# Top-k attention and SwiGLU FFN: attention straight through for nine units, the first block by halves, rounding in two VectorE steps

## The chip, the core and the metric

The kernel runs on one core of one Trainium2 chip. Its engines are named as in the profile: PE (TensorE, with PEld for its weight loads), DVE (VectorE), ACT (ScalarE), POOL (GpSimd) and SP (SyncE, which issues all transfers here). The metric is the device time in microseconds (us); lower is better. The time before is the median of three runs. A profile is one further execution; its span runs from its first to its last instruction.

## What is computed

Attention in which each query keeps its 32 highest scores, over 8 batches, 8 heads, 576 positions and head size 64; then a SwiGLU FFN on the 4608 x 512 result.

```python
scores = scale * np.matmul(q, k.transpose(0, 1, 3, 2))
kth = np.partition(scores, -top_k, axis=-1)[..., -top_k:-top_k + 1]
scores = np.where(scores >= kth, scores, -1000000000.0)
scores = scores - np.max(scores, axis=-1, keepdims=True)
attn = np.exp(scores)
attn = attn / (np.sum(attn, axis=-1, keepdims=True) + 1e-09)
x = bridge(np.matmul(attn, v))          # (B,H,S,D) -> (B*S, H*D)
g = x @ w_gate
silu = g * (1.0 / (1.0 + np.exp(-g)))
out = (silu * (x @ w_val)) @ w_out      # 4608x512 @ 512x1536, then 1536x512
```

The three weight matrices arrive as 64-bit floats and are brought to float32 inside the kernel, by integer operations on their two halves.

## The kernel before

**Units.** The attention is cut into 160 units, in the order batch, query tile, pair of heads: 8 batches, five query tiles (four of 128 queries, one of 64), four head pairs. A unit of a full tile does two heads one after the other on 128 partitions; a unit of the last tile holds both heads on the partition halves and counts as one head.

**One iteration of the main loop** (L523) selects for unit n on DVE, and carries its neighbours through the later stages on the other engines:

- `select(n)` (L264): four rounds of `max` (L277, the 8 highest) with three `match_replace` between them (L281), then one tensor_scalar (L287) that writes a penalty to `e` for every score below the 32nd. These eight steps are called one by one, with other work issued between them.
- `penalize(n-1)` (L291): on POOL, `e` + scores (L299). `weigh(n-1)` (L302): the exponential with its sum on ACT (L308). `normalize(n-1)` (L314): an addition and a reciprocal on DVE (L318, L320), and two multiplications on ACT (L323), which are issued at the start of the next iteration.
- `scores(n+1)` (L226): matrix products, copied out of PSUM by ACT.
- `turn(n-2)` (L325): nine transposes of `e` on PE with three copies on ACT (L336). `values(n-3)` (L346): attention times V, copied by ACT into `xT` (L379).
- `fetch(n+2)` (L492): transposes K and Q of a new head pair, or loads the next ones.

So unit n is finished in iteration n+3.

**FFN.** A block is 256 columns (tokens) of `xT`; 18 blocks. `feed(kb)` (L404) does it in 36 pieces: 24 of four matmul instructions (L418; two pieces make one product of 256 rows of gate or value) and 12 of two (L452, the output). A float32 matmul instruction shows as two records in the trace. Behind each product stand ACT instructions (L436 to L438 for a gate, L443 for a value) and a multiplication on POOL (L439, L444); they are kept in the lists `on_act` and `on_pool` and issued by later calls. `pieces(n)` issues up to n pieces if `credit` allows: each iteration adds 4.6 (2.3 for a unit of the last tile), at most 8.0 are kept. A block is begun when all its columns are there: block 0 needs units 0 to 7, block 1 units 8 to 15. What is left after the last unit runs in `while piece()` (L571).

**Rounding the weights.** The weights come in 72 pieces of 128 x 256 (`weights`, L129). Each goes through `rounded` (L92) in stages, and `rounding(k)` makes k steps; step i issues the load of piece i, the ACT and POOL part of piece i-3, the first DVE part of piece i-4 with POOL's addition, and the last DVE part of piece i-5. A step has three DVE instructions (L114, L117, L124), two on POOL (L102, L121) and two on ACT (L107, L109). In the first ten iterations there are five steps an iteration, two of them side by side, then four. `need` makes steps at once when a product wants a piece that isn't ready.

**Loads.** Before the loop, K and Q of the first four head pairs (`load`, six transfers each) and V (`load_v`, four each) are queued on SP, with three weight loads among them.

**Order.** The last loop (L579) chains every instruction of PE, DVE, ACT and POOL to the one issued before it: each engine works in the order in which the program issues. So an instruction that waits holds everything behind it on its engine.

Of the kernel before, what the change touches and what calls it, by code (L numbers as in the profile page):

```python
# [15 lines left out]
P = 128  # L16
# [4 lines left out]
BLK = 256  # L21
WP = 256
HUGE = 122880.0
LEAST = 3.4332275390625e-05


@with_exitstack
def kernel(
# [63 lines left out]
    def rounded(src, dst):  # L92

        n = dst.shape[1]
        w = ffn.tile([P, n, 2], I32, tag="w", name="w", bufs=4)
        nc.sync.dma_start(w[:], src.bitcast(I32).rearrange("p (f t) -> p f t", t=2))
        yield
        low, high = w[:, :, 0], w[:, :, 1]


        hi = conv.tile([P, n], FP32, tag="hi", name="hi")
        nc.gpsimd.tensor_scalar(  # L102
            hi[:], high.bitcast(FP32), HUGE, -HUGE, ALU.min, ALU.max
        )

        ulps = conv.tile([P, n], I32, tag="ulps", name="ulps")
        nc.scalar.mul(ulps[:], low.bitcast(U32), 2.0**-29)  # L107
        size = conv.tile([P, n], FP32, tag="size", name="size")
        nc.scalar.activation(size[:], hi[:], AF.Abs)  # L109
        yield  # L110

        hi = hi[:].bitcast(I32)
        bits = conv.tile([P, n], I32, tag="bits", name="bits")
        nc.vector.tensor_scalar(  # L114
            bits[:], hi, 3, 0x3FFFFFFF, ALU.logical_shift_left, ALU.bitwise_and
        )
        nc.vector.scalar_tensor_tensor(  # L117
            out=bits[:], in0=hi, scalar=-0x40000000, in1=bits[:],
            op0=ALU.bitwise_and, op1=ALU.bitwise_or,
        )  # L120
        nc.gpsimd.tensor_tensor(bits[:], bits[:], ulps[:], ALU.add)  # L121
        yield

        nc.vector.scalar_tensor_tensor(  # L124
            out=dst, in0=size[:], scalar=LEAST, in1=bits[:].bitcast(FP32),
            op0=ALU.is_ge, op1=ALU.mult,
        )

    def weights():  # L129
# [134 lines left out]
    def select(n):  # L264

        nh = n_heads(units[n][1])
        sc = state[n]["sc"]
        m = small.tile([P, 2, TOP_K], FP32, tag="m", name="m")
        heads = [slice(t * S, (t + 1) * S) for t in range(nh)]
        rest = work.tile([P, 2 * S], FP32, tag="rest", name="rest", bufs=1)  # L270
        e = work.tile([P, 2 * S], FP32, tag="e", name="e", bufs=3)
        state[n] |= dict(m=m, e=e, heads=heads)
        cur = sc
        rounds = TOP_K // 8
        for r in range(rounds):
            for t, hs in enumerate(heads):
                nc.vector.max(m[:, t, 8 * r : 8 * r + 8], cur[:, hs])  # L277
# [126 lines left out]
    def feed(kb):  # L404

        x = xT.pop(kb)
        hs = []  # L410

        def product(w, s, then):
            ps = ps_f.tile([P, 2, BLK], FP32, tag="f", name="f")
            need(8 * s + (4 if w is wg else 8))
            for i in range(2):
                m = 2 * s + i
                for c in range(KC):
                    nc.tensor.matmul(  # L418
                        ps[:, i, :],
                        w[:, c, m * P : (m + 1) * P],  # L420
                        x[:, c, :],
                        start=(c == 0),
                        stop=(c == KC - 1),
                    )
                if i == 1:
                    on_act.append(lambda: then(ps))
                yield

        for s in range(MS):
            h = ffn.tile([P, 2, BLK], FP32, tag="h", name="h", bufs=MS + 1)  # L430
            hs.append(h)


            def gate(ps, h=h):
                half = ffn.tile([P, 2, BLK], FP32, tag="gv", name="half_g", bufs=3)
                nc.scalar.activation(h[:], ps[:], AF.Tanh, scale=0.5)  # L436
                nc.scalar.mul(half[:], ps[:], 0.5)
                nc.scalar.add(h[:], h[:], 1.0)  # L438
                on_pool.append(lambda: nc.gpsimd.tensor_mul(h[:], h[:], half[:]))  # L439

            def value(ps, h=h):
                val = ffn.tile([P, 2, BLK], FP32, tag="gv", name="val", bufs=3)
                nc.scalar.copy(val[:], ps[:])  # L443
                on_pool.append(lambda: nc.gpsimd.tensor_mul(h[:], h[:], val[:]))  # L444

            yield from product(wg, s, gate)
            yield from product(wv, s, value)
        for t in range(BLK // P):
            ps = ps_f.tile([P, DM], FP32, tag="f", name="o_ps")
            for m in range(MC):  # L450
                need(8 * MS + 2 * m + 2)
                nc.tensor.matmul(  # L452
                    ps[:],
                    hs[m // 2][:, m % 2, t * P : (t + 1) * P],
                    wo[:, m, :],
                    start=(m == 0),
                    stop=(m == MC - 1),
                )
                if m == MC - 1:

                    def finish(ps=ps, t=t):
                        o = ffn.tile([P, DM], FP32, tag="o", name="o")
                        nc.scalar.copy(o[:], ps[:])
                        store(o, kb * BLK + t * P)

                    on_act.append(finish)
                if m % 2 == 1:
                    yield

    NU = len(units)  # L470
    todo = list(range(NBLK))
# [2 lines left out]
    def piece():  # L474

        if len(on_act) > 1:
            flush(on_act)
        if len(on_pool) > 1:
            flush(on_pool)
        while True:  # L480
            if not current:
                if not todo or done.get(todo[0], 0) < NHP * BLK:
                    return False
                flush(on_act)
                flush(on_pool)
                current.append(feed(todo.pop(0)))
            if next(current[0], 0) == 0:
                current.pop()
                continue
            return True  # L490

    def fetch(n):  # L492

# [5 lines left out]
            load(i + NHP)  # L499

    def pieces(n):
        for _ in range(n):
            if credit[0] >= 1 and piece():
                credit[0] -= 1

    def run(steps):
        for _ in steps:
            pass

    load(0)  # L510
    rounding(3)
    load(1)
    for i in range(NHP):
        if i > 1:
            load(i)
        load_v(i)
    run(fetch(0))
    run(scores(0))
    run(fetch(1))
    credit = [0.0]  # L520
    no = iter(())
    over = {}
    for n in range(NU + 3):  # L523
        topk = select(n) if n < NU else no
        over[n - 1] = normalize(n - 1) if 0 <= n - 1 < NU else no
        nxt = scores(n + 1) if n + 1 < NU else no
        turned = turn(n - 2) if 0 <= n - 2 < NU else no
        ahead = fetch(n + 2) if n + 2 < NU else no
        if n < NU:
            credit[0] = min(credit[0] + (2.3 if units[n][1] == J else 4.6), 8.0)  # L530
        flush(on_act)
        if 0 <= n - 1 < NU:
            penalize(n - 1)
        run(over.pop(n - 2, no))
        flush(on_pool)
        if n >= 3:
            values(n - 3)
            b, qt, hp = units[n - 3]
            if qt == J and b + 1 < B:
                load_v((b + 1) * NHP + hp)  # L540
        next(nxt, None)
        next(topk, None)
        next(topk, None)
        rounding(1 + (n < 2 * NHP + 2))
        pieces(1)
        next(nxt, None)
        next(turned, None)
        flush(on_act)
        pieces(1)
        next(turned, None)  # L550
        flush(on_act)
        if 0 <= n - 1 < NU:
            weigh(n - 1)
        flush(on_pool)
        next(topk, None)
        next(topk, None)
        rounding(1)
        next(ahead, None)
        pieces(1)
        next(ahead, None)  # L560
        next(topk, None)
        rounding(1)
        next(over[n - 1], None)
        pieces(1)
        next(topk, None)
        rounding(1)
        next(over[n - 1], None)
        next(topk, None)
        next(topk, None)
        pieces(6)  # L570
    while piece():  # L571
# [49 lines left out]
```

## Time and profile before

| | us |
|---|---|
| median of 3 runs (lowest, highest) | 1972.86 (1972.39, 1973.78) |
| the profiled execution | 1975.04 |
| its span | 1973.2 |
| PE busy | 1779.5 |
| DVE busy | 1640.1 |
| ACT busy | 1156.0 |
| POOL busy | 773.0 |

A line of the timeline gives start, length, engine, source line, operation, names and shapes; in brackets the idle time of the engine before it and what ended that. A line of the table by stages gives the stretch, its length, each engine's busy time and number of instructions, the clock granted to PE (1.00 is full), and the share and rate of DMA. The page draws the span in 40 slices of 49.3 us, a digit being tenths:

```profile
PE   3444779989999999999999999989999999899899
DVE  5999687998889998989799898998898988889700
POOL 2555453424334434343434352434343434243412
PEclk6566789999999999999999999999999999999999
DMA  5222111100030002100030002000120002000000
```

### The profile page before, as it was taken

Reading aid. Unit: us, or ns where it says so; the run is one execution under the profiler, and the core shown is the slowest. Engines: PE = TensorE matmul, PEld = TensorE weight load, DVE = VectorE, ACT = ScalarE, POOL = GpSimd, SP = SyncE. Lnnn points to the kernel's source line nnn. Section 1 sums busy time; section 2 is a strip of 40 time slices with the busy share of each in tenths; the row PEclk is TensorE's granted clock in tenths of the full one; section 3 lists DMA queues with packets and bytes.
Section 4 is the critical chain, followed back from the end, with each engine's and each line's share of the span. In section 5 each row is a group of like instructions: output and inputs, shape, how many; then the busy total and the mean of one; then the engine's idle time right before and its main releaser. Section 6 shows DMA issues by size and latency. Waiting matters only on the chain.

```text
span 1973.2 us, 29487 instructions
## 1 busy us (share of the span) xinstructions
PE 1779.5 (90%) x10144; PEld 1297.7 (66%) x10144; DVE 1640.1 (83%) x3708; ACT 1156.0 (59%) x2821; POOL 773.0 (39%) x686
## 2 busy tenths in 40 slices
PE   3444779989999999999999999989999999899899
PEld 1223655847686867686768686858686867586666
DVE  5999687998889998989799898998898988889700
ACT  3555455656575656666667566656675656565512
POOL 2555453424334434343434352434343434243412
PEclk6566789999999999999999999999999999999999
DMA  5222111100030002100030002000120002000000
GB/s 153 84 80 75 43 50 43 44 12 1 9 79 11 1 12 57 30 1 11 4 78 7 12 2 68 18 11 1 33 54 11 1 14 50 11 1 11 1 11 11
DMA packets 111253, 59.58 MB, mean 30 GB/s; under 512 B 89088, under 2 KB 97280, under 8 KB 111104
## 3 DMA queue, kind: packets, MB, share of 16 engines
q1 hardware_dynamic: 111104, 57.70, 11.1%
q8 instruction: 80, 1.31, 0.3%
q14 instruction: 69, 0.57, 0.1%
HBM read 48.23 MB, written 9.44 MB: 29 GB/s over the span
## 4 chain that ended last, share of the span: by engine, by line
PE 78%; DVE 13%; issue 3%; ACT 3%; POOL 2%; SPq 1%; DMA 1%; POOLq 0%; ACTq 0%; DVEq 0%
PE f L418 37%; PE o_ps L452 18%; PE av L364 7%; PE etps L335 6%; PE s L256 6%; DVE m L277 5%; DVE rest L281 4%; PE s L242 2%; PE av L355 1%; PE kqps L211 1%; DVE bits L117 1%; DVE e L287 1%; DVE bits L114 1%; ACT e L308 1%; POOL bits L121 1%
## 5 line engine op out<-in xcount | busy, mean ns | idle before, releaser
L299 POOL TENSOR_TENSOR e<-e,sc 128x1152 f32<-128x1152 f32 (+1 forms) x160 | 383.0, 2394 | 731.3 <-DVE e L287 487.1
L277 DVE MAX8 m<-rest 128x8 f32<-128x576 f32 x864 | 613.7, 747 | 2.2
L418 PE MATMUL f<-xT,wg 128*128 128x256 f32 x1728 | 423.1, 391 | 16.7 <-ACT xT L379 16.7
L281 DVE MATCH_REPLACE8 rest<-m,rest 128x576 f32<-128x576 f32 x576 | 423.9, 743 | 0.0
L418 PE MATMUL f<-xT,wv 128*128 128x256 f32 x1728 | 409.3, 384 | 0.0
L452 PE MATMUL o_ps<-wo,h 128*128 128x512 f32 x864 | 400.1, 599 | 4.4 <-DVE wo L124 4.4
L418 PEld LDWEIGHTS f<-xT,wg 128*128 128x128 f32 x1728 | 323.4, 194 | 89.7 <-issue 27.8
L336 ACT COPY et<-etps 128x512 f32<-128x512 f32 (+1 forms) x448 | 195.1, 477 | 305.8 <-PE etps L335 305.2
L418 PEld LDWEIGHTS f<-xT,wv 128*128 128x128 f32 x1728 | 321.0, 193 | 48.3 <-issue 9.9
L335 PE MATMUL etps<-ident,e 128*128 128x128 f32 (+1 forms) x1312 | 207.4, 289 | 122.2 <-ACT sc L261 70.5
L335 PEld LDWEIGHTS etps<-ident,e 128*128 128x128 f32 (+1 forms) x1312 | 168.0, 148 | 202.8 <-issue 99.1
L323 ACT ACTIVATE e<-e,tot 128x576 f32<-128x576 f32 x288 | 209.5, 770 | 133.7 <-DVE tot L320 133.7
L452 PEld LDWEIGHTS o_ps<-wo,h 128*128 128x128 f32 x864 | 153.6, 190 | 163.6 <-issue 156.0
L439 POOL TENSOR_TENSOR h<-h,half_g 128x512 f32<-128x512 f32 x108 | 137.9, 1277 | 265.3 <-ACT h L438 258.8
L308 ACT ACTIVATE e<-e,bias 128x576 f32<-128x576 f32 x288 | 221.6, 776 | 4.1 <-POOL e L299 4.1
L277 DVE MAX8 m<-sc 128x8 f32<-128x576 f32 x288 | 205.1, 749 | 10.1 <-ACT sc L261 10.1
L281 DVE MATCH_REPLACE8 rest<-m,sc 128x576 f32<-128x576 f32 x288 | 212.0, 743 | 0.0
L256 PE MATMUL s<-kqT 64*128 64x288 f32 x1024 | 172.7, 459 | 11.4 <-ACT kqT L216 11.3
L364 PE MATMUL av<-et,v 128*64 128x128 f32 (+1 forms) x2560 | 178.5, 281 | 2.1 <-ACT et L336 1.0
L261 ACT COPY sc<-s 128x288 f32<-128x288 f32 x512 | 167.2, 416 | 12.8 <-PE s L256 12.3
L318 DVE TENSOR_SCALAR tot<-tot 128x2 f32<-128x2 f32 (+1 forms) x160 | 25.4, 159 | 168.0 <-ACT e L308 168.0
L444 POOL TENSOR_TENSOR h<-h,val 128x512 f32<-128x512 f32 x108 | 139.1, 1288 | 60.7 <-ACT val L443 60.3
(45 smaller groups left out, 1459.8 us busy)
## 6 DMA issues: line engine op xcount, KB each, us to landing
kq_in<-in_k_dram SPq DMA_DIRECT2D x64, 128.0 KB, 2.8
kq_in<-in_q_dram SPq DMA_DIRECT2D x64, 128.0 KB, 3.0
v<-in_v_dram SPq DMA_DIRECT2D x32, 256.0 KB, 3.0
w<-in_moe_w_gate_dram SPq DMA_DIRECT2D x24, 256.0 KB, 2.7
w<-in_moe_w_val_dram SPq DMA_DIRECT2D x24, 256.0 KB, 2.7
w<-in_moe_w_out_dram SPq DMA_DIRECT2D x24, 256.0 KB, 2.5
out_dram<-o SPq DMA_DIRECT2D x40, 128.0 KB, 2.4
out_dram<-o SPq DMA_DIRECT2D x16, 256.0 KB, 2.4
```

The source lines that it names most:

```text
L256: nc.tensor.matmul(ps[:, 0:half], slab[d, q0 : q0 + P], slab[d, k0 : k0 + half])
L261: nc.scalar.copy(sc[:, i * half : (i + 1) * half], ps[:, 0:half])
L277: nc.vector.max(m[:, t, 8 * r : 8 * r + 8], cur[:, hs])
L281: nc.vector.match_replace(rest[:, hs], m[:, t, 8 * r : 8 * r + 8], cur[:, hs], LOWEST)
L299: nc.gpsimd.tensor_tensor(e[:, every], e[:, every], sc[:, every], ALU.add)
L308: nc.scalar.activation(e[:, hs], e[:, hs], AF.Exp, bias=bias[:, t : t + 1], scale=scale, accum_out=tot[:, t : t + 1],)
L323: nc.scalar.mul(e[:, hs], e[:, hs], tot[:, t : t + 1])
L335: nc.tensor.transpose(ps[0:kl, c * P : (c + 1) * P], e[:, k0 : k0 + kl], ident[:])
L336: nc.scalar.copy(et[0:kl, c0 : c0 + cn, :], ps[0:kl, 0 : cn * P].rearrange("p (c j) -> p c j", c=cn),)
L364: nc.tensor.matmul(av[hh * R : (hh + 1) * R, 0:ql], v_last[:, hh, :] if c == J else vt[:, hh, c, :], moving, start=last and c == 0, stop=c ...
L418: nc.tensor.matmul(ps[:, i, :], w[:, c, m * P : (m + 1) * P], x[:, c, :], start=(c == 0), stop=(c == KC - 1),)
L452: nc.tensor.matmul(ps[:], hs[m // 2][:, m % 2, t * P : (t + 1) * P], wo[:, m, :], start=(m == 0), stop=(m == MC - 1),)
```

## The change

- **Rounding.** The clamp moves behind the absolute value: ACT takes the absolute value first (L101 of the new kernel), POOL clamps it between LEAST and HUGE (L103), DVE shifts and masks (L110), POOL adds (L114), and one DVE instruction (L117) puts sign and top bit back from the loaded data. DVE has two instructions a step instead of three. LEAST is 2^-15 now. A loaded piece is held until its last step, and its ring has six buffers instead of four.
- **Steps.** In the first nine iterations (`head`) there are five calls of `rounding` instead of four, the new one between the first `max` and the first `match_replace`; each makes two steps in iterations 0 to 4, one after that. Four steps are made before the loop instead of three.
- **Straight through.** In the first nine iterations, unit n-1 is normalized, turned, multiplied with V and finished at the end of iteration n. Units from 8 on go the old way.
- **First block by halves.** Block 0 begins when units 0 to 3 are done, with its first 128 columns: 24 pieces of half width, then the same for the other 128 columns when units 4 to 7 are done, then the 12 output pieces. Half-width pieces count half.
- **Credit.** 8.0 is added in each of the first nine iterations, and at most 10.0 are kept, in all iterations.
- **Loads.** Before the loop only the first two head pairs' K and Q are loaded; the other two in iterations 0 and 1, V in iterations 1 to 4.
- The ring of `m` has two buffers instead of three. Before the seventh output matmul, what is left in `on_act` and `on_pool` is issued.

```diff
-LEAST = 3.4332275390625e-05
+LEAST = 3.0517578125e-05
...
-        w = ffn.tile([P, n, 2], I32, tag="w", name="w", bufs=4)
+        w = ffn.tile([P, n, 2], I32, tag="w", name="w", bufs=6)
...
-        hi = conv.tile([P, n], FP32, tag="hi", name="hi")
-        nc.gpsimd.tensor_scalar(
-            hi[:], high.bitcast(FP32), HUGE, -HUGE, ALU.min, ALU.max
-        )
+        size = conv.tile([P, n], FP32, tag="size", name="size")
+        nc.scalar.activation(size[:], high.bitcast(FP32), AF.Abs)
+
+        nc.gpsimd.tensor_scalar(size[:], size[:], HUGE, LEAST, ALU.min, ALU.max)
 
         ulps = conv.tile([P, n], I32, tag="ulps", name="ulps")
         nc.scalar.mul(ulps[:], low.bitcast(U32), 2.0**-29)
-        size = conv.tile([P, n], FP32, tag="size", name="size")
-        nc.scalar.activation(size[:], hi[:], AF.Abs)
         yield
 
-        hi = hi[:].bitcast(I32)
         bits = conv.tile([P, n], I32, tag="bits", name="bits")
         nc.vector.tensor_scalar(
-            bits[:], hi, 3, 0x3FFFFFFF, ALU.logical_shift_left, ALU.bitwise_and
-        )
-        nc.vector.scalar_tensor_tensor(
-            out=bits[:], in0=hi, scalar=-0x40000000, in1=bits[:],
-            op0=ALU.bitwise_and, op1=ALU.bitwise_or,
+            bits[:], size[:].bitcast(I32), 3, 0x3FFFFFFF,
+            ALU.logical_shift_left, ALU.bitwise_and,
         )
         nc.gpsimd.tensor_tensor(bits[:], bits[:], ulps[:], ALU.add)
         yield
 
         nc.vector.scalar_tensor_tensor(
-            out=dst, in0=size[:], scalar=LEAST, in1=bits[:].bitcast(FP32),
-            op0=ALU.is_ge, op1=ALU.mult,
+            out=dst.bitcast(I32), in0=high, scalar=-0x40000000, in1=bits[:],
+            op0=ALU.bitwise_and, op1=ALU.bitwise_or,
         )
...
-        m = small.tile([P, 2, TOP_K], FP32, tag="m", name="m")
+        m = small.tile([P, 2, TOP_K], FP32, tag="m", name="m", bufs=2)
...
+        halves = [slice(0, P), slice(P, BLK)] if kb == 0 else [slice(0, BLK)]
+        for c in halves:
+            while done[kb] < NHP * c.stop:
+                yield 0
+            for s in range(MS):
...
+                yield from product(wg, s, c, gate)
+                yield from product(wv, s, c, value)
...
+                if m == 6:
+                    flush(on_act)
+                    flush(on_pool)
...
-                if not todo or done.get(todo[0], 0) < NHP * BLK:
-                    return False
+                if not todo or done.get(todo[0], 0) < NHP * (BLK if todo[0] else P):
+                    return 0
...
     load(0)
-    rounding(3)
+    rounding(4)
     load(1)
-    for i in range(NHP):
-        if i > 1:
-            load(i)
-        load_v(i)
...
+    HEAD = 2 * NHP + 1
     for n in range(NU + 3):
+        head = n < HEAD
...
-        turned = turn(n - 2) if 0 <= n - 2 < NU else no
+        turned = turn(n - 2) if HEAD - 1 <= n - 2 < NU else no
         ahead = fetch(n + 2) if n + 2 < NU else no
+        ticks = 2 if n < NHP + 1 else 1
         if n < NU:
-            credit[0] = min(credit[0] + (2.3 if units[n][1] == J else 4.6), 8.0)
+            new = 8.0 if head else 2.3 if units[n][1] == J else 4.6
+            credit[0] = min(credit[0] + new, 10.0)
...
-        if n >= 3:
-            values(n - 3)
...
+        if n - 3 >= HEAD - 1:
+            finish_unit(n - 3)
         next(nxt, None)
         next(topk, None)
-        next(topk, None)
-        rounding(1 + (n < 2 * NHP + 2))
+        if head:
+            rounding(ticks)
+            if 2 <= n + 2 < NHP:
+                load(n + 2)
+            if 0 <= n - 1 < NHP:
+                load_v(n - 1)
+        next(topk, None)
+        rounding(ticks)
...
         next(over[n - 1], None)
-        next(topk, None)
+        if head:
+            run(over.pop(n - 1))
+            pieces(1)
+            if n >= 1:
+                run(turn(n - 1))
+        next(topk, None)
+        if head:
+            pieces(1)
+            if n >= 1:
+                finish_unit(n - 1)
         next(topk, None)
         pieces(6)
```

`finish_unit(n)` is the old `values(n)` with the load of V that followed it; the three other calls of `rounding` in an iteration have `ticks` in place of 1.

More of the change, by code (lines that the diff above doesn't have):

```diff
@@ L404, in feed, with product @@
     def feed(kb):
-        x = xT.pop(kb)
+        x = xT[kb]
         hs = []
-        def product(w, s, then):
+        def product(w, s, c, then):
+            n = c.stop - c.start
             ps = ps_f.tile([P, 2, BLK], FP32, tag="f", name="f")
@@ L416, in product @@
                 m = 2 * s + i
-                for c in range(KC):
+                for kc in range(KC):
                     nc.tensor.matmul(
[L419 to L423, printed above, removed]
+                        ps[:, i, 0:n],
+                        w[:, kc, m * P : (m + 1) * P],
+                        x[:, kc, c],
+                        start=(kc == 0),
+                        stop=(kc == KC - 1),
@@ L424, in product @@
                     )
                 if i == 1:
[L426 to L447, printed above, removed]
+                    on_act.append(lambda: then(ps[:, :, 0:n], c))
@@ new lines, in product, with gate, value @@
+                yield n / BLK
+        halves = [slice(0, P), slice(P, BLK)] if kb == 0 else [slice(0, BLK)]
[3 more added lines that the diff above has]
+            for s in range(MS):
+                if c.start == 0:
+                    hs.append(ffn.tile([P, 2, BLK], FP32, tag="h", name="h", bufs=MS + 1))
+                h = hs[s]
+                def gate(ps, c, h=h):
+                    half = ffn.tile([P, 2, BLK], FP32, tag="gv", name="half_g", bufs=3)
+                    hc, gc = h[:, :, c], half[:, :, c]
+                    nc.scalar.activation(hc, ps, AF.Tanh, scale=0.5)
+                    nc.scalar.mul(gc, ps, 0.5)
+                    nc.scalar.add(hc, hc, 1.0)
+                    on_pool.append(lambda: nc.gpsimd.tensor_mul(hc, hc, gc))
+                def value(ps, c, h=h):
+                    val = ffn.tile([P, 2, BLK], FP32, tag="gv", name="val", bufs=3)
+                    hc, vc = h[:, :, c], val[:, :, c]
+                    nc.scalar.copy(vc, ps)
+                    on_pool.append(lambda: nc.gpsimd.tensor_mul(hc, hc, vc))
+                yield from product(wg, s, c, gate)
+                yield from product(wv, s, c, value)
@@ L448, in feed @@
+        del xT[kb]
         for t in range(BLK // P):
@@ L467, in feed @@
                 if m % 2 == 1:
-                    yield
+                    yield 1
     NU = len(units)
@@ L486, in piece @@
                 current.append(feed(todo.pop(0)))
[L487 to L490, printed above, removed]
+            size = next(current[0], None)
+            if size is not None:
+                return size
+            current.pop()
     def fetch(n):
@@ L501, in pieces @@
     def pieces(n):
-        for _ in range(n):
-            if credit[0] >= 1 and piece():
-                credit[0] -= 1
+        while n > 0 and credit[0] >= 1:
+            size = piece()
+            if not size:
+                break
+            n -= size
+            credit[0] -= size
     def run(steps):
@@ L508, in run, with finish_unit @@
             pass
+    def finish_unit(n):
+        values(n)
+        b, qt, hp = units[n]
+        if qt == J and b + 1 < B:
+            load_v((b + 1) * NHP + hp)
     load(0)
-    rounding(3)
+    rounding(4)
     load(1)
-    for i in range(NHP):
-        if i > 1:
-            load(i)
-        load_v(i)
     run(fetch(0))
@@ L535 @@
         flush(on_pool)
-        if n >= 3:
-            values(n - 3)
-            b, qt, hp = units[n - 3]
-            if qt == J and b + 1 < B:
-                load_v((b + 1) * NHP + hp)
+        if n - 3 >= HEAD - 1:
+            finish_unit(n - 3)
         next(nxt, None)
         next(topk, None)
+        if head:
[4 more added lines that the diff above has]
+                load_v(n - 1)
         next(topk, None)
-        rounding(1 + (n < 2 * NHP + 2))
+        rounding(ticks)
         pieces(1)
@@ L556 @@
         next(topk, None)
-        rounding(1)
+        rounding(ticks)
         next(ahead, None)
@@ L561 @@
         next(topk, None)
-        rounding(1)
+        rounding(ticks)
         next(over[n - 1], None)
@@ L565 @@
         next(topk, None)
-        rounding(1)
+        rounding(ticks)
         next(over[n - 1], None)
+        if head:
[3 more added lines that the diff above has]
+                run(turn(n - 1))
         next(topk, None)
+        if head:
+            pieces(1)
+            if n >= 1:
+                finish_unit(n - 1)
         next(topk, None)
```

## The prediction

> **What bounds the kernel now.** I read the busy time by stage first, cut at the ends of the L287 instructions that close loop iterations 0, 4, 8, 9, 11, 17, 29 and 159. Columns: length; busy time of PE, PEld, DVE, ACT, POOL; granted clock; DMA.
>
> ```profile
> 0.00:35.60 35.60, 13.31 (x55) 8.17 (x55) 14.80 (x38) 12.46 (x32) 6.03 (x16) 0.77 0.63 165
> 35.60:103.70 68.10, 25.88 (x118) 16.72 (x118) 62.51 (x157) 34.67 (x93) 35.76 (x48) 0.57 0.33 94
> 103.70:171.80 68.10, 29.70 (x140) 19.50 (x140) 62.51 (x158) 35.99 (x97) 35.77 (x48) 0.60 0.27 78
> 171.80:188.80 17.00, 8.96 (x41) 5.97 (x41) 15.60 (x41) 8.96 (x25) 8.95 (x12) 0.60 0.23 79
> 188.80:234.00 45.20, 34.23 (x168) 27.79 (x168) 31.95 (x74) 22.37 (x57) 21.38 (x25) 0.85 0.15 47
> 234.00:327.70 93.70, 71.50 (x344) 47.43 (x345) 74.67 (x169) 48.44 (x121) 43.03 (x48) 0.82 0.11 36
> 327.70:454.40 126.70, 115.32 (x699) 85.42 (x698) 118.89 (x268) 79.93 (x202) 45.25 (x36) 0.95 0.14 35
> 454.40:1871.70 1417.30, 1385.90 (x8223) 1022.78 (x8222) 1258.87 (x2812) 892.12 (x2160) 557.68 (x438) 1.00 0.08 21
> 1871.70:1973.20 101.50, 94.72 (x360) 63.95 (x358) 0.32 (x2) 21.11 (x41) 19.14 (x15) 0.94 0.05 11
> ```
>
> From 454 us on PE is busy 1385.9 of 1417.3 us at full clock, and then 94.7 of 101.5: matrix work is the bound there. Before 172 us VectorE is: 62.5 of 68.1 us in four iterations, 17.02 each. Counting FFN pieces in the order of instructions, both programs have issued 72 of 648 by the end of iteration 29 (before 35, after 36 by the end of 17), because block 1 (units 8 to 15) can start only in iteration 18 in both. So the same 576 pieces are left at 454 us, and the forecast is what iterations 0 to 29 cost. Next I read the stalls of VectorE, in its order of time: two rounding steps put side by side; two other places; and the first iteration.
>
> ```profile
> 106.40 0.41 DVE L124 SCALAR_TENSOR_TENSOR wv<-size,bits 128x256 f32<-128x256 f32 x1
> 106.73 0.28 DVE L114 TENSOR_SCALAR bits<-hi 128x256 int32<-128x256 int32 x1
> 107.05 0.42 DVE L117 SCALAR_TENSOR_TENSOR bits<-hi,bits 128x256 int32<-128x256 int32 x1
> 108.40 0.42 DVE L124 SCALAR_TENSOR_TENSOR wg<-size,bits 128x256 f32<-128x256 f32 x1 [0.93 <-POOL bits L121]
> 109.12 0.29 DVE L114 TENSOR_SCALAR bits<-hi 128x256 int32<-128x256 int32 x1 [0.30 <-POOL hi L102]
> ...
> 109.80 1.42 DVE L277 MAX8 m<-rest 128x8 f32<-128x576 f32 x2
> ```
> ```profile
> 203.72 0.63 DVE L124 SCALAR_TENSOR_TENSOR wo<-size,bits 128x256 f32<-128x256 f32 x1 [6.02 <-POOL bits L121]
> ...
> 213.15 2.72 DVE L117 SCALAR_TENSOR_TENSOR bits<-hi,bits 128x256 int32<-128x256 int32 x1
> ```
> ```profile
> 201.73 1.28 POOL L439 TENSOR_TENSOR h<-h,half_g 128x512 f32<-128x512 f32 x1 [7.74 <-ACT h L438]
> 202.96 0.73 POOL L121 TENSOR_TENSOR bits<-bits,ulps 128x256 int32<-128x256 int32 x1
> ...
> 212.93 2.66 POOL L299 TENSOR_TENSOR e<-e,sc 128x1152 f32<-128x1152 f32 x1
> ```
> ```profile
> 32.66 0.29 DVE L114 TENSOR_SCALAR bits<-hi 128x256 int32<-128x256 int32 x1 [9.76 <-POOL hi L102]
> ```
>
> A pair lasts 3.40 us (106.40 to 109.80), a lone step about 1.0 (15.63 busy of an iteration less 10.63 of an iteration without steps, over five). So a pair waits some 1.4 us on POOL: the last VectorE step of one piece needs POOL's addition for it, issued in the same pair. At 203.72 VectorE lost 6.02 us: the addition stood in POOL's queue behind an FFN multiplication, which waited on ACT, and ACT on PE. At 32.66 it lost 9.76 us to a weight load queued on SP behind the loads of V.
>
> **The change part by part** (t counts from an iteration's start).
>
> *A step.* VectorE keeps one tensor_scalar and one two-input step, by their start-to-start distances 0.32 and 0.33: 0.65 instead of 1.0 us. A pair is then 0.33 + 0.28 to the end of its first shift, 0.17 + 0.72 until POOL has added (L117's end to POOL's start, and L121), 0.04 to the second two-input step; POOL's clamp behind it 0.64 (as at 108.45, beside L124; 0.41 alone), and a last shift of 0.32: 2.5 us. Bounds: 1.3 with no wait, 3.4 as now. I take 2.5.
>
> *Iteration 0.* ACT's absolute value and ulps of the first piece now precede the copies of kqT, and POOL now takes that piece at 8.21 us: first maximum at 13.6 instead of 11.5. The 9.76 us wait goes (V is loaded later), five pairs come: 13.6 + 10.63 + 5 x 2.5 = 36.7 less 0.3, for the first pair lacks a step. Against 35.6: **+0.8**.
>
> *Iterations 1 to 4*, five pairs each. The first pair stands at t = 1.33, straight under POOL's addition of e (0.23 to 2.86). Besides, ACT now ends the previous unit first: from the reciprocal (2.35 before the iteration's end) two multiplications of 0.72, transposes (1.09 for four at the low clock), three copies, av (0.80 + 1.98), the copy to xT: 6.5 us, so t = 4.15. Only then comes the absolute value, 0.42, clamp, shift: the pair ends at 5.6 and costs 4.25. Sum 10.63 + 4.25 + 4 x 2.5 = 24.9 (between 17.1 without waits and 27.6 with pairs as now), four times +7.9: **+31.5**.
>
> The Trainium skill (SBUF — State Buffer, "Who interferes with whom") says that a VectorE instruction with two SBUF inputs and a GpSimd instruction that reads SBUF exclude each other, the later one blocking whole. The trace agrees: L117 at 213.15 took 2.72 us instead of 0.42 and ended at 215.87, just after L299's end at 215.59. The rule speaks against this change: by it the 0.23 us that the clamp loses beside each two-input step stays, some 5.7 us over 25 pairs; without it the sum would be 5.7 lower.
>
> *Iterations 5 and 6.* Twelve half-width pieces, six products, are issued at the end of iteration 4, and their 12 ACT instructions and 6 POOL multiplications stand ahead of the next absolute value and addition. A whole product takes 3.45 us (16 records, 1906.64 to 1910.09), one with 512 columns 0.4325 a record (48 in 20.76): time goes with the columns, so a half product is 1.73 or more, at most 16 x 0.154 = 2.46 by the transposes (five in 0.77). I take 1.9, near the first. PE is free at about t = 3.9; the first product at half clock, five more: 17.2. Then ACT 0.6, POOL's remaining multiplication, addition and clamp behind the delayed 2.63 us addition of e: VectorE's second step ends at 20.2. What is left is 7.85 of selection, three steps, 0.5 of waits: 30.5 (15.4 without that queue; 34 at 2.46). In iteration 6 the other six products and the late unit 4 hold ACT until t = 10.5: 10.5 + 9.8 = 20.3. Against 17.02: **+13.5, +3.3**. Iterations 7 and 8: 10.63 + 5 x 0.65 + 1.5 for a second step behind the late absolute value = 15.4: **-3.2**.
>
> *Iterations 9 to 11.* Block 0's other half repeats this in 9, with fewer steps: 29 against 17.0, **+12**. In 10 VectorE's sum of e waits for an exponential behind six products and the first output pieces (1.73 each): 17 against 20.95 (188.8 to 209.8 us), **-4**; 11: 12.4 against 24.2, **-11.8**.
>
> *Iterations 12 to 17* have no matmul pieces left: four at 10.63 and two at 6.03 against 74.8 (234.0 to 308.8 us) and 18.9 (to 327.7): **-32.3, -6.9**.
>
> *Iterations 18 to 29.* Both do block 1. The higher cap on credit bunches ten pieces into iteration 18, where the clock has to rise again, and block 1 ends an iteration earlier, so that four instead of three iterations run at 10.63 with little beside them. Bounds 0 and +10.6 (one such iteration, unhidden); half: **+5**.
>
> *At nothing:* the later loads of K and Q (6 issues of 0.64 us each) and of V (4) are used half an iteration later or more; a weight piece has two pairs, 7 us, against 3.5 for issue and landing. Without that cover the steps wait on SP. The ring of two for m, the extra flush, the other LEAST: POOL reads m an iteration before it is written again, the flush finds mostly empty queues, and a constant costs no time. The cap also leaves 53 instead of 55 pieces behind the last unit, but those two run where PE is full: 0 (at best -3.5).
>
> Sum: 0.8 + 31.5 + 13.5 + 3.3 - 3.2 + 12 - 4 - 11.8 - 32.3 - 6.9 + 5 = **+7.9**: the span goes from 1973.2 to 1981.1, the profiled execution from 1975.04 to 1983, and the median of 1972.86, to which I add the same, to **1981**.
>
> **The rivals.**
> - *The early half of block 0 falls into idle PE time*, PE being busy under half of iterations 1 to 8. Then iterations 5, 6, 9, 10 cost 15.4, 15.4, 14.2 and 14: 38 us less, **1943**, faster. It decides if the additions in 5 and 9 come by t = 10 rather than 20. The wait of 6.02 behind a single product speaks against it.
> - *Pairs wait on nothing*: 25 times 1.2 less, **1951**. The 0.93 and 0.30 speak against it.
> - *The same terms, smaller stalls*: products at 1.73, no cost in 18 to 29: about 8 less, **1973**, no change.
> - *Weight loads late*: a load now waits for the last step of the piece six before it, and in iterations 0 and 1 stands behind loads on SP. One more us in each of 20 pairs: **2001**. SP's landing of 2.7 us speaks against it.
>
> **How the numbers follow.** My forecast 0.50 (1977 to 1997), late loads and other queues 0.13, no change 0.14, idle PE time 0.13, free pairs 0.10. About 0.2%, 4 us, is what a measurement of this kernel can tell from no change; faster is 0.23, same 0.14, slower 0.63. The range 1957 to 2000 leaves out some 2 in 10, mostly the two fast rivals.
>
> **What would show it.** Iterations 1 to 4 near 25 us, with VectorE idle before each second two-input step on POOL's addition; iterations 5 and 9 near 30, idle on the same addition behind multiplications; iterations 12 to 15 at 10.63; the stretch behind iteration 29 unchanged within 4 us. I am wrong if 5 and 9 stay under 20, or 1 to 4 under 20.

## The result and the profile after

The changed kernel takes 1991.59 us (median of 4 runs, 1988.58 to 1995.4) against 1972.8 before: 18.8 us slower, ratio 1.0095 with a 95% interval of 1.0075 to 1.0116. The forecast was slower by 8, to 1981: the right side, and less than half the size. The profiled execution is the slowest of the four, 1995.4 us with a span of 1993.3, so differences read in the trace add up to 20.1 instead of 18.8.

This is the table by stage of the changed kernel, cut at the ends of the same iterations as the one in the prediction (columns as there):

```profile
0.00:34.80 34.80, 14.53 (x55) 8.82 (x55) 17.50 (x46) 17.14 (x45) 12.54 (x28) 0.82 0.70 184
34.80:128.60 93.80, 19.85 (x116) 15.73 (x117) 74.52 (x177) 54.34 (x135) 56.75 (x87) 0.59 0.48 138
128.60:207.20 78.60, 45.24 (x334) 40.39 (x333) 57.14 (x138) 45.08 (x121) 42.99 (x60) 0.74 0.17 58
207.20:232.40 25.20, 25.20 (x216) 24.02 (x215) 12.30 (x31) 12.22 (x37) 12.04 (x15) 0.95 0.00 1
232.40:260.80 28.40, 28.40 (x132) 15.37 (x131) 21.52 (x50) 14.49 (x36) 7.26 (x7) 1.00 0.03 10
260.80:316.40 55.60, 32.95 (x216) 23.32 (x216) 54.58 (x123) 30.89 (x77) 15.69 (x12) 0.85 0.03 8
316.40:455.30 138.90, 117.43 (x696) 87.36 (x695) 118.82 (x267) 80.07 (x200) 45.20 (x36) 0.91 0.12 30
455.30:1895.60 1440.30, 1399.78 (x8239) 1033.29 (x8238) 1259.19 (x2812) 894.08 (x2163) 558.40 (x439) 0.99 0.08 21
1895.60:1993.30 97.70, 91.10 (x345) 60.85 (x343) 0.35 (x3) 19.48 (x38) 17.87 (x14) 0.94 0.05 11
```

Beside the table of before, the lengths differ by -0.8, +25.7, +10.5, +8.2, -16.8, -38.1, +12.2, **+23.0** and -3.8 us. The first eighteen iterations go much as the prediction says: more in iterations 1 to 9, given back in 10 to 17. At the end of iteration 29 the changed kernel stands 0.9 us behind (455.3 against 454.4). Nearly the whole loss comes after that, in the 130 iterations where the prediction had booked nothing.

What waits there is seen in VectorE's timeline, in iteration 31 (467.4 to 487.3 us); the block of FFN in front of it is begun in iteration 30, as soon as unit 27 is done. First the changed kernel, then the one before (in brackets the idle time ahead of the instruction):

```profile
483.41 0.17 DVE L311 TENSOR_SCALAR tot<-tot 128x2 f32<-128x2 f32 x1 [9.13 <-ACT e L301]
```
```profile
478.39 0.17 DVE L318 TENSOR_SCALAR tot<-tot 128x2 f32<-128x2 f32 x1 [6.50 <-ACT e L308]
```

VectorE waits for the sum of the exponentials, 9.13 us instead of 6.50. ACT's timeline of the changed kernel tells what the exponential stood behind:

```profile
473.74 0.60 ACT L437 ACTIVATE h<-f 128x512 f32<-128x512 f32 x1 [2.81 <-PE f L412]
...
478.51 0.75 ACT L329 COPY et<-etps 128x512 f32<-128x512 f32 x2 [0.50 <-PE etps L328]
480.79 0.58 ACT L329 COPY et<-etps 128x512 f32<-128x512 f32 x1 [1.52 <-PE etps L328]
481.27 0.59 ACT L445 COPY val<-f 128x512 f32<-128x512 f32 x1
481.75 0.79 ACT L301 ACTIVATE e<-e,bias 128x576 f32<-128x576 f32 x1
```

ACT was waiting for PE, and PE was working through the ten pieces that the credit had let into one iteration (eight before). Three of PE's lines from the same time, FFN products between the transposes and scores of attention:

```profile
470.08 3.62 PE L412 MATMUL f<-xT,wg 128*128 128x256 f32 x16
476.05 1.99 PE L412 MATMUL f<-xT,wv 128*128 128x256 f32 x8
478.42 1.89 PE L412 MATMUL f<-xT,wv 128*128 128x256 f32 x8
```

Between the ends of iterations 29 and 159 VectorE waits 174.2 us for the exponential (L301) in the changed kernel, at most 9.1 at once, and 150.9, at most 6.7, in the kernel before (L308 there): 23.3 us more, as much as the stretch grows. Six iterations wait most, each behind the start of a block: 31, 67, 75, 111, 147 and 155. They last 19.7 to 19.9 us each instead of 17.2 to 17.4, in sum 118.9 instead of 103.7, and PE is busy all through them. The other 124 iterations take 7.9 us more together.

### The profile page after: what moved, and what is told of

Its sections match the earlier page's. It is cut to its first block, busy times and chain, and to the rows that moved or that the text cites. A ratio compares the mean times of both kernels' runs of the same rounds, so it can differ in the third digit from the quotient of the medians.

```text
span 1993.3 us, 29774 instructions
## 1 busy us (share of the span) xinstructions
PE 1774.5 (89%) x10336; PEld 1309.2 (66%) x10336; DVE 1615.9 (81%) x3636; ACT 1167.8 (59%) x2845; POOL 768.7 (39%) x698
## 4 chain that ended last, share of the span: by engine, by line
PE 78%; DVE 13%; ACT 4%; issue 3%; POOL 2%; DMA 0%; SPq 0%; DVEq 0%; POOLq 0%; ACTq 0%
PE f L412 37%; PE o_ps L458 18%; PE etps L328 7%; PE av L357 6%; PE s L249 6%; DVE rest L274 5%; DVE m L270 5%; PE s L235 2%; POOL bits L114 1%; PE av L348 1%; ACT e L301 1%; PE kqps L204 1%; DVE e L280 1%; ACT et L329 1%; DVE bits L110 1%
## 5 line engine op out<-in xcount | busy, mean ns | idle before, releaser
L292 POOL TENSOR_TENSOR e<-e,sc 128x1152 f32<-128x1152 f32 (+1 forms) x160 | 382.4, 2390 | 789.2 <-DVE e L280 515.0
L412 PE MATMUL f<-xT,wg 128*128 128x256 f32 (+1 forms) x1824 | 414.4, 375 | 20.6 <-ACT xT L372 20.6
L412 PE MATMUL f<-xT,wv 128*128 128x256 f32 (+1 forms) x1824 | 412.8, 374 | 0.0
L301 ACT ACTIVATE e<-e,bias 128x576 f32<-128x576 f32 x288 | 221.9, 777 | 10.9 <-POOL e L292 10.9
L440 POOL TENSOR_TENSOR h<-h,half_g 128x512 f32<-128x512 f32 (+1 forms) x114 | 138.7, 1217 | 196.5 <-ACT h L439 193.0
L270 DVE MAX8 m<-sc 128x8 f32<-128x576 f32 x288 | 205.1, 749 | 11.4 <-ACT sc L254 11.4
L446 POOL TENSOR_TENSOR h<-h,val 128x512 f32<-128x512 f32 (+1 forms) x114 | 138.6, 1216 | 140.7 <-ACT val L445 139.0
L357 PE MATMUL av<-et,v 128*64 128x128 f32 (+1 forms) x2560 | 182.5, 283 | 2.5 <-ACT et L329 1.0
L249 PE MATMUL s<-kqT 64*128 64x288 f32 x1024 | 166.2, 445 | 14.8 <-ACT kqT L209 14.6
L254 ACT COPY sc<-s 128x288 f32<-128x288 f32 x512 | 167.4, 418 | 18.9 <-PE s L249 18.4
```

The source lines that it names most:

```text
L249: nc.tensor.matmul(ps[:, 0:half], slab[d, q0 : q0 + P], slab[d, k0 : k0 + half])
L254: nc.scalar.copy(sc[:, i * half : (i + 1) * half], ps[:, 0:half])
L292: nc.gpsimd.tensor_tensor(e[:, every], e[:, every], sc[:, every], ALU.add)
L301: nc.scalar.activation(e[:, hs], e[:, hs], AF.Exp, bias=bias[:, t : t + 1], scale=scale, accum_out=tot[:, t : t + 1],)
L357: nc.tensor.matmul(av[hh * R : (hh + 1) * R, 0:ql], v_last[:, hh, :] if c == J else vt[:, hh, c, :], moving, start=last and c == 0, stop=c ...
L412: nc.tensor.matmul(ps[:, i, 0:n], w[:, kc, m * P : (m + 1) * P], x[:, kc, c], start=(kc == 0), stop=(kc == KC - 1),)
```

## The experiments

Three theories were open for the stretch after iteration 29: the larger cap on credit; the smaller ring of m or the extra flush; and the prediction's own step, that the two pieces that the cap moves cost nothing, in which case the loss would need another source. The later runs ask what the head's own stalls cost.

**e1_cap8: the changed kernel with the old cap.**

```diff
-            credit[0] = min(credit[0] + new, 10.0)
+            credit[0] = min(credit[0] + new, 8.0)
```

> The changed kernel, but at most 8.0 of credit kept instead of 10.0. Cap theory: behind iteration 29 the ten-piece bursts at the start of a block (VectorE idle 9.1 us on the exponential, where the kernel before idles 6.5) cost the 19 us; then 1973 us (1968 to 1978), waits of 6.5 at the block starts, and the stretch behind iteration 29 as long as in the kernel before (1417 to the last selection). Ring-and-flush theory (the smaller ring of m or the extra flush costs them): still 1988 to 1995. The prediction's own step, that the two pieces cost nothing: within 4 us of 1991.6.

Measured: 1973.05 us, ratio to the kernel before 0.9997 (0.9987 to 1.0006). One number takes away the 18.5 us; all the rest of the change together is worth nothing that can be measured. The wait at the block's start is 6.68 us again.

**e2_before_cap10: the kernel before with the new cap.** Its edit is the reverse, 8.0 to 10.0. In this kernel and in e7 the last multiplication of block 16 on POOL (L444) comes behind the output matmuls that read its result (here at 1920.50 us, they from 1899.56), so a part of that block's output is wrong. The instructions are the same in number and shape, so the two runs serve for their time alone; the flush ahead of the seventh output matmul, which the changed kernel has, keeps the order.

> The kernel before, with 10.0 of credit kept instead of 8.0 and nothing else. Cap theory: 1991 us (1985 to 1997), some 18 more than before, with VectorE idle about 9 us at the block starts. Ring-and-flush theory, and the prediction's step: 1973, within 4 us.

Measured: 1990.56 us, ratio 1.0092 (1.0074 to 1.0109). The cap alone makes the kernel before as slow as the changed one. The waits of the six iterations are 8.95 to 9.13 us, as in the changed kernel.

**e3_ring_flush: the kernel before with the two small edits that work in every block.**

```diff
-        m = small.tile([P, 2, TOP_K], FP32, tag="m", name="m")
+        m = small.tile([P, 2, TOP_K], FP32, tag="m", name="m", bufs=2)
...
+                if m == 6:
+                    flush(on_act)
+                    flush(on_pool)
```

> The kernel before, with the ring of m at two buffers and the flush ahead of the seventh output matmul, and nothing else. Cap theory: 1973 us, within 4. Ring-and-flush theory: 1985 to 1992.

Measured: 1974.75 us, ratio 1.0005 (0.9996 to 1.0014). They cost nothing, and that theory is out.

**e4_lag: the changed kernel, the stages of a weight piece further apart.** A pair's second step no longer needs what POOL does for the first.

```diff
-        for n in range(len(pieces) + 5):
-            for lag in (5, 4, 3, 0):
+        for n in range(len(pieces) + 6):
+            for lag in (6, 4, 2, 0):
...
-            ready[0] = max(n - 4, 0)
+            ready[0] = max(n - 5, 0)
```

> The changed kernel, with the stages of rounding two steps apart (6, 4, 2, 0 instead of 5, 4, 3, 0), so that no DVE instruction of a pair waits for POOL's work of the same pair. Pair theory: the waits of 0.90 and 0.29 us in each of 25 pairs go, 1.2 us each; iterations 1 to 4 take 18.7 instead of 23.4 us, and with iteration 0 some 25 to 30 us less arrive at the end: 1965 us (1960 to 1972). Rival, that the first block's products decide the head anyway: iteration 5 grows by what 1 to 4 lose, and the time stays over 1985.

Measured: 1985.5 us, ratio 1.0065 (1.0049 to 1.0082): 6 us gained, where 25 were expected and none by the rival. Neither holds. The waits did go, but iterations 1 to 4 take 21.1 to 21.9 us, not 18.7. Iteration 3 in VectorE's timeline, and the same moment on POOL:

```profile
80.81 0.41 DVE L117 SCALAR_TENSOR_TENSOR wv<-w,bits 128x256 int32<-128x256 int32 x1
81.33 0.63 DVE L110 TENSOR_SCALAR bits<-size 128x256 int32<-128x256 int32 x1
81.87 0.61 DVE L117 SCALAR_TENSOR_TENSOR wv<-w,bits 128x256 int32<-128x256 int32 x1
82.59 0.63 DVE L110 TENSOR_SCALAR bits<-size 128x256 int32<-128x256 int32 x1
```
```profile
80.86 0.94 POOL L114 TENSOR_TENSOR bits<-bits,ulps 128x256 int32<-128x256 int32 x1
81.77 0.44 POOL L103 TENSOR_SCALAR size<-size 128x256 f32<-128x256 f32 x1
82.18 0.89 POOL L114 TENSOR_TENSOR bits<-bits,ulps 128x256 int32<-128x256 int32 x1
```

The shift takes 0.63 us instead of 0.28, the two-input step 0.61 instead of 0.42, POOL's addition 0.94 instead of 0.72: with the semaphore wait gone, the two engines' instructions fall on each other and lengthen. Over iterations 1 to 4 VectorE's idle time falls by 15.1 us (19.3 to 4.2) and its busy time grows by 7.5 (74.5 to 82.1): half of the wait became length.

**e5_spread_cap8: cap 8.0, and fewer pieces at once in the head.**

```diff
-            credit[0] = min(credit[0] + new, 10.0)
+            credit[0] = min(credit[0] + new, 8.0)
...
-        pieces(6)
+        pieces(2 if n < HEAD + 3 else 6)
```

> The changed kernel with 8.0 of credit kept and, in iterations 0 to 11, at most two pieces (four of half width) instead of six behind an iteration's last selection. Queue theory: iterations 5 and 9 lose 13.6 and about 11 us because the addition of a rounding step stands behind four to six FFN multiplications; with fewer of them in front iterations 5, 6, 9 and 10 together take some 15 us less than the 86 they take with a cap of 8.0, and the time is 1958 us (1953 to 1964). Rival, that block 0's matrix work itself bounds the head: iterations 7 and 10 to 13 grow by as much, 1968 to 1975.

Measured: 1961.69 us, ratio 0.9941 (0.9924 to 0.9957), 11.4 us better than e1. Iterations 5, 6, 9 and 10 take 71.9 us instead of 85.7 (27.29, 20.02, 25.71 and 12.71 in e1; 19.70, 20.74, 18.32 and 13.12 here); iterations 7, 11 and 12 grow by 4.3, and iteration 29 ends 9.9 us earlier (438.3 against 448.2). VectorE's waits of this kind (L117 for wo on POOL) fall from 33.1 to 18.0 us in sum: not quite half of that wait was made by the order of issue, and the rest is still there.

**e6_lag_spread_cap8: e5 with e4's stages.**

> The same with the stages of rounding two steps apart (6, 4, 2, 0). If the gains add: the six us that the wider stages gave before come on top of the kernel with the spread, 1952 us (1946 to 1958). Rival, that the wider stages only turn waits into longer VectorE instructions wherever POOL is busy: within 3 us of that kernel.

Measured: 1959.75 us, ratio 0.9927 (0.9912 to 0.9942). 1.9 us less than e5, within 3 as the rival has it: iterations 1 to 4 win some 8 us, and iterations 5 to 9 give 6.4 of it back, most in 6 and 9 (23.20 and 20.17 instead of 20.74 and 18.32).

**e7_before_cap6: the kernel before, cap 6.0.**

> The kernel before, with 6.0 of credit kept instead of 8.0. Burst theory: an iteration that starts a block takes 4.1 us of attention on PE and 1.73 for each piece kept, against 10.63 on VectorE; with six pieces 14.5 instead of 17.2 us, six times, and 3.5 us more behind the last unit: 1960 us (1955 to 1967). Rival, that eight was already below what matters and only ten hurts: within 4 us of 1973; or that the pieces missed come back at the end in full: over 1980.

Measured: 1957.22 us, ratio 0.9913 (0.9898 to 0.9928). The burst theory's 1960, a little better: eight was too many as well.

**e8_lag_spread_cap6: e6, cap 6.0 after the head.** The cap is 10.0 in the first nine iterations and 6.0 behind them.

> The changed kernel with the spread, the wider stages and, behind the first nine iterations, 6.0 of credit kept. If the three effects add: 1940 us (1933 to 1950), better than both kernels. If the cap's effect ends at 8.0: 1952.

Measured: 1934.16 us, ratio 0.9797 (0.9783 to 0.9812). The effects add, and some more.

**e9_cap5: e8 with 5.0.**

> The kernel with spread, wider stages and cap 6.0, with 5.0 of credit kept behind the first nine iterations. Burst theory: an iteration that starts a block with five pieces takes 12.8 us instead of 14.5, some six times, and one piece more, 1.7 us, stands behind the last unit: 1926 us (1920 to 1932). Rival, that the pieces missed collect behind the last unit or that another wait takes over: 1934 or more.

Measured: 1917.81 us, ratio 0.9708 (0.9694 to 0.9723): 16.4 us less than e8, where 8 were expected. Here is the stretch from the end of iteration 29 to that of 159 by cap: e1 (8.0), e8 (6.0), e9 (5.0); the changed kernel (10.0) is the eighth line of the first table.

```profile
448.20:1867.10 1418.90, 1387.51 (x8224) 1023.96 (x8222) 1258.91 (x2813) 891.48 (x2160) 557.12 (x438) 0.99 0.08 21
```
```profile
427.10:1825.80 1398.70, 1379.83 (x8206) 1019.49 (x8205) 1259.05 (x2813) 890.20 (x2159) 555.84 (x437) 1.00 0.08 21
```
```profile
424.90:1810.40 1385.50, 1373.69 (x8200) 1015.47 (x8200) 1259.99 (x2813) 893.08 (x2159) 556.13 (x437) 1.00 0.09 21
```

1440.3, 1418.9, 1398.7 and 1385.5 us, with nearly the same matmul records in each (39 fewer at 5.0 than at 10.0). The other edits of e8 and e9 act in the first twelve iterations only; e12, the kernel before with 5.0, takes 1385.4 too. What is left behind the last unit grows only from 97.7 (10.0) through 101.5 and 103.8 to 106.1 us. PE is "busy" for 97 to 99% of the stretch in all four. Its idle time, 40.5, 31.4, 18.9 and 11.8 us, accounts for 28.7 of the 54.8 us between the caps of 10.0 and 5.0. Its busy time falls by the other 26.1: some 8 us by the 39 records (an estimate, at the 0.216 us a record of a whole product), the rest with a clock a little higher (0.99 against 1.00) and not taken apart. In the six iterations behind a block's start VectorE's wait for the exponential is 8.95 to 9.13 us at 10.0, 6.45 to 6.68 at 8.0, 1.99 to 2.22 at 6.0 and none at 5.0, where they last 10.7 us.

**e10_fewer_pairs: e5 with fewer steps side by side.**

```diff
-        ticks = 2 if n < NHP + 1 else 1
+        ticks = iter((1, 2, 1, 2, 2) if n < 6 else (1,) * 5)
...
-            rounding(ticks)
+            rounding(next(ticks))
```

> The changed kernel with cap 8.0 and the spread (stages as in the changed kernel), with 1, 2, 1, 2, 2 steps at the five places of iterations 0 to 5 and 1 at each in 6 to 8, instead of 2 at each in 0 to 4 and 1 after that: the step under POOL's addition of e is alone, and seven pairs fewer are made in all. Pair theory: 1.2 us for each pair less and up to 1.8 for each of the first places: iterations 1 to 4 at some 19.5 instead of 23.4 us, iteration 5 3 us longer; 1950 us (1944 to 1956) against 1961.7. Rival, that a lone step there waits as long on POOL: 1959 to 1962.

Measured: 1950.46 us, ratio 0.9875 (0.9859 to 0.9892), 11.2 less than e5. Iterations 1 to 4 take 19.79 to 19.87 us each, iteration 5 takes 25.67, 6 us longer than in e5 where 3 were expected. The total and the price of a pair come out as expected.

**e11_best: e10's head, and 5.0 after it.**

> The kernel with the spread and fewer pairs, and 5.0 of credit kept behind the first nine iterations instead of 8.0. If head and cap add: 1917.8 for cap 5.0 less the 9.3 by which fewer pairs beat the wider stages at a cap of 8.0: 1908.5 us (1904 to 1914). If they share one gain: 1915 or more.

Measured: 1915.54 us, ratio 0.9700 (0.9684 to 0.9716), 2.3 less than e9 and not 9.3. The two share a gain: in e9 the cap of 5.0 also holds in iterations 9 to 11 and shortens them to 18.90, 10.63 and 11.15 us (20.17, 13.16 and 13.78 in e6); in e11 they are 20.93, 13.67 and 11.51, near those of e10. By this the lead of the head with fewer pairs falls from 5.2 us at the end of iteration 9 to 1.8 at the end of 11 (between e6 and e10 it is 5.1 there): about half of the missing 7 us; where the rest goes was not traced. It is the best version tried, 3.0% under the kernel before.

**e12_before_cap5: the kernel before, cap 5.0, with both edits of e3.**

> The kernel before with the flush ahead of the seventh output matmul and 5.0 of credit kept instead of 8.0, its first iterations as they were. Burst theory: two steps of some 16 us as between 8.0, 6.0 and 5.0 in the other kernels: 1941 us (1934 to 1948). Against the kernel with the new head at the same cap (1908 expected) it tells what the head is worth: over 25 us if the head's gain is carried to the end, under 10 if it isn't.

Measured: 1939.31 us, ratio 0.9821 (0.9807 to 0.9836). Against e11 at the same cap the new head, spread and with fewer pairs, is worth 23.8 us, and at the end of iteration 29 it leads by 24.8 (421.6 against 446.4): what the head gains is carried to the end, though 23.8 is just short of the 25 that was named for it.

## Why the prediction fell short

**The step that failed** is the last one under "At nothing": that the cap leaves 53 instead of 55 pieces behind the last unit, "but those two run where PE is full: 0 (at best -3.5)". The -3.5 came (97.7 against 101.5 us behind the last unit). The 0 was +23.0. The two pieces run behind a block's start, six times in the stretch, where they keep ACT, and so the exponential, waiting 2.3 to 2.6 us longer each time. Ahead of a block PE then runs dry: in iterations 64, 65 and 73, before the starts felt in 67 and 75, it idles 11.9 us, and 5.2 in e1. The reading behind the 0 was "PE is busy 1385.9 of 1417.3 us at full clock", hence "matrix work is the bound there". Runs with nearly the same matrix work finish that stretch in 1385.5: the share of 98% is an average. In the kernel before PE is busy throughout the six iterations of 17.2 to 17.4 us, while 45 of the 130 iterations take 10.63 us, and in these VectorE is busy throughout; the two engines bind in turn. e1, e2 and e3 settle from both sides that the cap is the cause.

**Iterations 18 to 29**, booked at +5 with bounds 0 and +10.6, took 12.2 more. It is a step of the same kind: the prediction has the ten pieces bunched in iteration 18, and prices them too low. Iteration 19 behind them lasts 20.10 us (7.92 before), with VectorE's longest wait for the exponential, 13.82 us; the other eleven iterations cancel out. The clock did not have to rise again: it is 1.00 in 18 and 19. Iteration 19 shortens with the cap, to 17.59 in e1, 13.19 in e8 (6.0) and 11.21 in e9 and e11 (5.0). It is short in the kernel before, at a cap of 8.0, because little credit is saved there: of the 8.0 at the start of block 0 in iteration 10 and the 27.6 added until 17, 35 pieces are issued. In the changed kernel almost no pieces are left for iterations 12 to 17, and the credit stands at the cap. On PE some 7.6 pieces start in iteration 19 there, and 3.0 in the kernel before.

**Iterations 0 to 17**, booked at +2.9, took 11.3 less. By term, forecast and measured: iteration 0 +0.8, -0.8; 1 to 4 +31.5, +25.7; 5 +13.5, +10.7; 6 +3.3, +4.4; 7 and 8 -3.2, -4.6; 9 +12, +8.2; 10 and 11 -15.8, -16.8; 12 to 17 -39.2, -38.1. Apart from iteration 0 every sign is right, and the stalls of 1 to 5 and 9 are smaller than forecast, that of 6 a little larger. Two pairs of iteration 2 of the changed kernel, VectorE's timeline:

```profile
59.47 1.74 DVE L117 SCALAR_TENSOR_TENSOR wg<-w,bits 128x256 int32<-128x256 int32 x1
61.13 0.28 DVE L110 TENSOR_SCALAR bits<-size 128x256 int32<-128x256 int32 x1
62.32 0.43 DVE L117 SCALAR_TENSOR_TENSOR wv<-w,bits 128x256 int32<-128x256 int32 x1 [0.90 <-POOL bits L114]
63.03 0.30 DVE L110 TENSOR_SCALAR bits<-size 128x256 int32<-128x256 int32 x1 [0.29 <-POOL size L103]
...
64.70 0.42 DVE L117 SCALAR_TENSOR_TENSOR wv<-w,bits 128x256 int32<-128x256 int32 x1
65.03 0.29 DVE L110 TENSOR_SCALAR bits<-size 128x256 int32<-128x256 int32 x1
66.22 0.61 DVE L117 SCALAR_TENSOR_TENSOR wv<-w,bits 128x256 int32<-128x256 int32 x1 [0.90 <-POOL bits L114]
66.75 0.28 DVE L110 TENSOR_SCALAR bits<-size 128x256 int32<-128x256 int32 x1
66.96 1.41 DVE L270 MAX8 m<-rest 128x8 f32<-128x576 f32 x2
```

The second pair runs from 64.70 to 66.96: 2.26 us, not 2.5, since the two-input step lost time beside POOL's clamp (0.61) and the clamp did not (0.40, where 0.64 was booked). The first, 59.47 to 63.24, is 3.77, not 4.25. Its first step lasts 1.74 instead of 0.42: it stands under POOL's addition of e and ends at 61.21, when that has ended.

The page SBUF — State Buffer of the Trainium skill, in "Who interferes with whom", has such an instruction with two inputs blocked whole by a GpSimd instruction that started first. The trace agrees: POOL's L292 ran from 58.30 to 60.92 us. The page also lists tensor_scalar among those that can take the shared pair, under conditions on their operands; e4 agrees there, with L110 at 0.63 us beside POOL's addition where it takes 0.28 alone.

The long waits came where they were forecast, on POOL's addition behind FFN multiplications. VectorE in the changed kernel, iterations 5, 6 and 9, and POOL up to the first of them:

```profile
145.53 0.42 DVE L117 SCALAR_TENSOR_TENSOR wo<-w,bits 128x256 int32<-128x256 int32 x1 [13.61 <-POOL bits L114]
...
167.31 0.42 DVE L117 SCALAR_TENSOR_TENSOR wo<-w,bits 128x256 int32<-128x256 int32 x1 [7.26 <-POOL bits L114]
...
224.12 0.42 DVE L117 SCALAR_TENSOR_TENSOR wo<-w,bits 128x256 int32<-128x256 int32 x1 [10.81 <-POOL bits L114]
```
```profile
139.74 0.72 POOL L446 TENSOR_TENSOR h<-h,val 128x256 f32<-128x256 f32 x1 [0.59 <-ACT val L445]
140.53 0.21 POOL L290 TENSOR_SCALAR bias<-m 128x2 f32<-128x2 f32 x1
140.70 2.63 POOL L292 TENSOR_TENSOR e<-e,sc 128x1152 f32<-128x1152 f32 x1
143.28 0.73 POOL L440 TENSOR_TENSOR h<-h,half_g 128x256 f32<-128x256 f32 x1
144.09 0.72 POOL L446 TENSOR_TENSOR h<-h,val 128x256 f32<-128x256 f32 x1
144.78 0.72 POOL L114 TENSOR_TENSOR bits<-bits,ulps 128x256 int32<-128x256 int32 x1
```

Four multiplications (the last at 139.74), the addition of e, two more multiplications, then the rounding's addition at 144.78: the queue that the prediction walked through, some 3 us quicker, as a half-width product took 1.79 us (PE from 135.40 to 137.18) instead of 1.9, and the first one 1.89 (131.72 to 133.61) where the prediction had it at half clock: the clock rose at once (it is 0.93 over iteration 5).

**The rivals.** Idle PE time and free pairs needed iterations 5 and 1 to 4 under 20 us; they were 27.7 and 23.4; the additions in 5 and 9 came at t = 16.2 and 16.1, neither by 10 nor at 20. Late loads needed waits on SP's transfers; VectorE shows none. The rival of no change was nearest for the first 455 us and is what e1 measures for the change without its cap.

**Still open.** Of the 21.4 us between caps 10.0 and 8.0 in the long stretch (the changed kernel and e1), 15.1 fall in the six iterations behind a block's start. The other 6 or so lie in the 124 iterations between; how much of them is PE's idle time and how much the lower clock was not taken apart. A cap below 5.0 was not run.

## What to carry to other kernels

Where one engine's filler work is released by a credit, the cap on what may be saved up sets the size of a burst, and in queues that work in order a burst delays whatever the bound engine needs next: here 2 of 10 pieces were worth 18.5 us, and 5.0 instead of 8.0 was worth 35 in the kernel before (e12 against e3). A PE that reads 98% busy over a long stretch says neither that PE is the bound throughout nor that work added there is free; move a piece and see whether the stretch moves. And when a wait between two engines is taken away, look whether the instructions themselves grow.

## What was not expected of the hardware

In e4 a one-input tensor_scalar of 128 x 256 int32 on VectorE grew from 0.28 to 0.63 us beside POOL's addition, and that addition from 0.72 to 0.94: both engines lost. And with PE busy 21 to 44% of the time the granted clock stays near 0.6 for as long as that lasts (0.57 over iterations 1 to 4 and 0.60 over 5 to 8 of the kernel before, 0.59 over 1 to 4 of the changed one), but with twelve half-width pieces in a row it was at 0.93 over the same iteration in which they began.
